# An mLSTM and two feed-forward layers on one core: state products of two batches in one group, a planner's constants, and the weights' conversion on VectorE and ScalarE alone

## The chip, the core and the metric

The kernel runs on one core of a Trainium2 chip. The core has TensorE for matrix products (PE in the profile, with its weight loads as PEld), VectorE (DVE), ScalarE (ACT), GpSimd (POOL) and SyncE (SP), which here issues every DMA. The metric is the device time of one execution in microseconds; less is better.

## The reference

A recurrence over 768 steps for 4 batches and 8 heads of size 40 gives `y`; two feed-forward layers of width 320 and inner width 2048 follow, all in float32.

```python
for t in range(S):                                  # S = 768, per batch and head
    m_new = maximum(f[t] + m, i[t])
    fs, is_ = exp(f[t] + m - m_new), exp(i[t] - m_new); m = m_new
    C = fs * C + is_ * outer(v[t], k[t])            # 40 x 40 state
    n = fs * n + is_ * k[t]
    y[t] = sigmoid(o_gate[t]) * (C @ q[t]) / maximum(abs(n @ q[t]), 1)
x = y.reshape(3072, 320)
h = x @ w_in1;  x = maximum(0.01 * h, h) @ w_out1   # layer 0
h = maximum(x @ w_in2, 0);  out = (h * h) @ w_out2  # layer 1
```

## The kernel before

**Work.** Time is cut into 6 chunks of 128 steps, and a chunk of all 4 batches is a block of 512 tokens. `attention(c)` computes a chunk in parallel form: for each of 8 groups `g` (a batch, four heads) decay factors (`ex_`, L626, then a triangular `affine_select` on GpSimd, L629), the products of keys and queries (`mS`, L635), their product with the factors on VectorE (L638), the product with the values (`mPV`, L651, or `mPV3` in three bf16 parts, L657 to L660), and from chunk 1 on the part from the state (`mI`, L645). For each batch the state is renewed: GpSimd weights the values (`wv`, L696), `mU` (L705) multiplies them with the keys for 8 heads into the PSUM tile `attm`, and VectorE adds (L719). Then come the gates (L732 to L739), a transposition (`mT`, L746) and the split of the block into a rounded and a low part, `xH` and `xL` (L752). Keys and values of a batch lie in a tile `nat` with two slots, `wv` has two slots too, and `attm` is one bank that `mU` and `mT` share.

**Feed-forward layers.** For each block and each of 16 slices `j` of the inner width, `moe_h` makes 8 products into `hp` (L435), ScalarE and VectorE make of it `gH` and its low part `gL` (L441 to L443, in layer 1 L446 to L449), and `out1` (L466 to L472) or `out2` (L514 to L516) adds its 8 or 12 products to accumulators. Chunk 0 of layer 0 is done in two halves of 256 tokens, the second seven slices behind the first, since its 16 weight slices arrive and are converted in the meantime.

**Conversion.** `weight(layer, j)` gets a slice as raw 64-bit words (704 KB) and makes a rounded and a low part: a shift and a merge on VectorE (L394, L396), a conversion of the low words on ScalarE (L398), an addition (L399), the rounding on ScalarE (L402), and subtractions for the low parts (`stack`, 64 x 128, L411; `sub`, L406, for layer 0 of 512 and of 64 columns). Addition and subtractions can go to VectorE or GpSimd: the planner decides by which is free first.

**Order.** Each operation is handed to `Sched` with an engine, an assumed duration and a key, the time in hundredths of a block at which it should come. `Sched.order` plays these operations through on a model of the engines, turns the plan into latest times, does so six times and keeps the best plan. Each engine then runs its instructions in that order. The keys are built from the numbers of `ORDER`: for instance `w0` and `ws` set those of the weights of layer 0, `c0` and `cs` those of the attention of the next chunk, `a04`, `a1` and others those of the first two chunks. While the planner finds nothing for TensorE early in the program, it places products of zeros (L322, L462, L479).

Of the kernel before, what the change touches and what calls it, by code (L numbers as in the profile page):

```python
# [19 lines left out]
E = 42  # L20
# [30 lines left out]
class Sched:  # L51
# [211 lines left out]
def mlstm_moe_kernel(  # L263
# [111 lines left out]
    def weight(layer, j, key):  # L375
        if layer == 0:
            raw = sb(f"x2_{(4, 5, 0, 1)[j % 4]}", [128, WR, 2], I32)
            if j < 2:
                fs[j] = sb(f"x2_{2 + j}", [128, 2, WR], I32)
            fb, fr = fs[j % 2], j // 2 % 2  # L380
        else:
            raw = sb(("T", "X")[j % 2], [128, WR, 2], I32)
            fb, fr = sb("qkr", [128, 1, WR], I32), 0
        ft = lambda: fb.t[:, fr]
        w = sb(f"w{j}", [128, WT], F32R)
        wt[layer, j] = w
# [4 lines left out]
        op("DVE", dve(WR, True), key, lambda: V.tensor_scalar(out=ft(), in0=hi(), scalar1=3, scalar2=0x3FFFFFFF, op0=ALU.logical_shift_left, op1=ALU.bitwise_and),  # L394
           r=[(raw, 0)], w=[(fb, fr)])
        op("DVE", dve(WR), key, lambda: V.scalar_tensor_tensor(out=ft(), in0=hi(), scalar=-0x40000000, in1=ft(), op0=ALU.bitwise_and, op1=ALU.bitwise_or),  # L396
           r=[(raw, 0), (fb, fr)], w=[(fb, fr)])
        op("ACT", act(WR), key - 0.1, lambda: A.activation(l.t, raw.t.bitcast(U32)[:, :, 0], AF.Copy, scale=2.0 ** -29), r=[(raw, 0)], w=[(l, 0)])  # L398
        add = lambda eng: eng.tensor_tensor(out=ft(), in0=ft(), in1=l.t, op=ALU.add)  # L399
        op("DVE", dve(WR), key, lambda: add(V), r=[(fb, fr), (l, 0)], w=[(fb, fr)], alt=("POOL", pool(WR), lambda: add(G)))  # L400
        f32 = lambda: ft().bitcast(F32)
        op("ACT", act(WR), key, lambda: A.copy(w.t[:, 0:WR], f32()), r=[(fb, fr)], w=[(w, "H"), (w, "C")])  # L402
        c0 = 512 if layer == 0 else 576

        def low(eng, o, n, s):
            eng.tensor_tensor(out=w.t[:, o:o + n], in0=f32()[:, s:s + n], in1=w.t[:, s:s + n].bitcast(F32), op=ALU.subtract)  # L406


        def stack(eng):
            c = w.t[64:128, c0:c0 + 128]  # L410
            eng.tensor_tensor(out=c, in0=f32()[64:128, c0:c0 + 128], in1=c.bitcast(F32), op=ALU.subtract)  # L411

        op("DVE", dve(128), key, lambda: stack(V), r=[(fb, fr), (w, "C")], w=[(w, "C")], alt=("POOL", pool(128), lambda: stack(G)))
        def sub(o, n, s0, w_):
            op("DVE", dve(n), key, lambda: low(V, o, n, s0), r=[(fb, fr), (w, "H")], w=w_, alt=("POOL", pool(n), lambda: low(G, o, n, s0)))

        if layer == 0:
            sub(768, 512, 0, [(w, "L")])
            sub(704, 64, 640, [(w, "Lc")])
        else:  # L420
            sub(704, 576, 0, [(w, "L"), (w, "Lc")])
# [108 lines left out]
    def attention(c, keys, ld):  # L530
# [31 lines left out]
        if c == 0:  # L562
            op("ACT", 100, -499, lambda: A.activation(act0.t, act0.t, AF.Exp), r=[(act0, 0)] + [(ogt, b) for b in range(B)], w=[(act0, 0)], table="exp")

        for b in range(B):
            kb = keys[2 * b] + (10 if c == 0 else 0)
            nt = sb("nat", [128, H * D + H * E], slots=2)
# [125 lines left out]
            if c < NCH - 1:  # L693
                kU = ko + (0.8 if c else 8 if b > 1 else 185)
                wv = sb("wv", [128, H, E], slots=2)
                mwv = lambda eng, wv=wv, v=v, b=b: eng.tensor_tensor(  # L696
                    out=wv.t, in0=v(), in1=ex.t[:, 1, 8 * b:8 * b + 8].unsqueeze(2).to_broadcast([128, H, E]), op=ALU.mult)
                op("POOL", 708, kU - 0.2, lambda mwv=mwv: mwv(G), r=[(nt, 0), (ex, 0)], w=[(wv, 0)])
                ks = kU + ORDER["ks"] if c == 0 else ko + 2
                up = ps("attm")  # L700

                def mU(up=up, wv=wv, nt=nt):
                    for h in range(H):
                        r, o = h % 2 * 64, h // 2 * E
# [3 lines left out]
                st = lambda b=b: C32.t[:, 8 * b:8 * b + 8]
                stk = lambda k, b=b: C32.t[:, 8 * b + k:8 * b + 8:2]
                u = lambda k, up=up: up.t[64 * k:64 * k + D, 0:H // 2 * E].rearrange("p (h e) -> p h e", e=E)  # L710
                if c == 0:
                    for k in range(2):
                        op("ACT", act(H // 2 * E, True), kU, lambda stk=stk, u=u, k=k: A.copy(stk(k), u(k)), r=[(up, 0)], w=[(C32, (b, k))])
                else:
                    op("POOL", 708, ko + 0.7, lambda st=st, b=b: G.tensor_tensor(
                        out=st(), in0=st(), in1=ex.t[0:D, 2, 8 * b:8 * b + 8].unsqueeze(2).to_broadcast([D, H, E]), op=ALU.mult),
                        r=[(ex, 0), (C32, (b, 0)), (C32, (b, 1))], w=[(C32, (b, 0)), (C32, (b, 1))])
                    for k in range(2):
                        op("DVE", dve(H // 2 * E), kU, lambda stk=stk, u=u, k=k: V.tensor_tensor(out=stk(k), in0=stk(k), in1=u(k), op=ALU.add),  # L719
                           r=[(up, 0), (C32, (b, k))], w=[(C32, (b, k))])  # L720
                if c + 1 >= NATIVE:
                    rb = slice(8 * b, 8 * b + 8)
                    CL = sb("CL", [D, H, E], F32R, 2)
                    op("ACT", act(H * E), ks, lambda st=st, rb=rb: A.copy(Cst.t[0:D, rb], st()), r=[(C32, (b, 0)), (C32, (b, 1))], w=[(Cst, (b, 0))])
                    op("DVE", dve(H * E), ks, lambda st=st, rb=rb, CL=CL: V.tensor_tensor(
                        out=CL.t, in0=st(), in1=Cst.t[0:D, rb].bitcast(F32), op=ALU.subtract), r=[(C32, (b, 0)), (C32, (b, 1)), (Cst, (b, 0))], w=[(CL, 0)])
                    op("SP", 800, ks, lambda rb=rb: SP.dma_start(out=Cst.t[2 * D:3 * D, rb].bitcast(F32), in_=Cst.t[0:D, rb].bitcast(F32)), r=[(Cst, (b, 0))], w=[(Cst, (b, 2))], lat=300)
                    op("SP", 800, ks, lambda rb=rb, CL=CL: SP.dma_start(out=Cst.t[D:2 * D, rb].bitcast(F32), in_=CL.t.bitcast(F32)), r=[(CL, 0)], w=[(Cst, (b, 1))], lat=300)
# [126 lines left out]
```

## Time and profile before

| | |
|---|---|
| median of 3 runs | 869.04 us (864.34 to 873.08) |
| profiled execution | 863.92 us, of which the span is 862.2 us |
| granted clock of TensorE, mean | 0.994 |
| TensorE busy | 843.5 us (98%) |
| VectorE, ScalarE, GpSimd busy | 540.1, 465.7, 115.1 us |

A row of the profile groups equal instructions: line, engine, operation, result and operands, count, then busy time and the mean of one in ns, then the idle time of the engine just before them and what ended it. The start of a matrix product is exact, its end is modelled; the time of a group of products is read from one group's start to the next.

### The profile page before, as it was taken

To read this page: it belongs to the slowest core of one execution; us is meant where nothing else is said; L and a number is where in the kernel's file an instruction comes from. 1 tells how busy PE (TensorE), PEld (TensorE's weight loads), DVE (VectorE), ACT (ScalarE), POOL (GpSimd) and SP (SyncE) were. 2 spreads that over 40 slices of the span, in tenths; PEclk is the share of its full clock that TensorE was granted. 3 is DMA by queue.
4 is the path that set the end of the run, shared out by engine and by line. 5 is a ranking of instruction groups with operands and counts; after the bars stand their busy time and mean duration, and the time that the engine had idled before them with its cause. 6 is when DMAs were issued, how large, how long until landed. Compare 5 with 4: busy or idle time off the path is not lost.

```text
span 862.2 us, 14025 instructions
## 1 busy us (share of the span) xinstructions
PE 843.5 (98%) x5307; PEld 723.9 (84%) x5311; DVE 540.1 (63%) x967; ACT 465.7 (54%) x946; POOL 115.1 (13%) x142
## 2 busy tenths in 40 slices
PE   9989999999999999999999999999999999999998
PEld 7788899777777778778777889999999999999997
DVE  5999946766866777667666899453443443533433
ACT  7577537755865685587546665443333433433332
POOL 2566614100310310011100000000000000000000
PEclk9899999999999999999999999999999999999999
DMA  8686224444444444452232442000000000000000
GB/s 226 215 264 196 70 62 153 137 128 126 142 132 131 140 130 133 129 163 94 93 115 100 136 160 76 1 31 1 1 31 1 0 32 1 31 1 1 32 1 31
DMA packets 52212, 78.61 MB, mean 91 GB/s; under 512 B 4336, under 2 KB 40784, under 8 KB 52144
## 3 DMA queue, kind: packets, MB, share of 16 engines
q1 hardware_dynamic: 52144, 77.71, 28.2%
q8 instruction: 42, 0.69, 0.3%
q14 instruction: 26, 0.21, 0.1%
HBM read 54.26 MB, written 4.01 MB: 68 GB/s over the span
## 4 chain that ended last, share of the span: by engine, by line
PE 76%; DVE 10%; ACT 5%; issue 3%; DMA 2%; SPq 2%; POOL 1%; ACTq 0%; POOLq 0%; DVEq 0%
PE hp L435 35%; PE acc L466 4%; PE acc L468 3%; PE acc L516 3%; PE acc L467 3%; PE acc L515 3%; PE acc L514 3%; SPq L581 2%; PE acc L471 2%; PE acc L472 2%; PE atty L645 2%; PE attS L635 2%; DVE aw L638 1%; PE atty L516 1%; PE atty L514 1%
## 5 line engine op out<-in xcount | busy, mean ns | idle before, releaser
L435 PE MATMUL hp<-xH,w 128*128 128x512 f32 (+1 forms) x1040 | 295.6, 381 | 6.9 <-DVE gL L443 3.6
L435 PEld LDWEIGHTS hp<-xH,w 128*128 128x128 f32 x1040 | 183.4, 189 | 38.3 <-DVE gL L443 5.5
L435 PE MATMUL hp<-xL,w 128*128 128x512 f32 (+1 forms) x624 | 198.6, 375 | 0.0
L447 DVE TENSOR_TENSOR g<-g 128x512 f32<-128x512 f32 x96 | 67.5, 704 | 117.9 <-ACT g L446 117.9
L435 PEld LDWEIGHTS hp<-xL,w 128*128 128x128 f32 x624 | 115.6, 189 | 22.4
L446 ACT ACTIVATE g<-hp 128x512 f32<-128x512 f32 x96 | 57.3, 597 | 128.9 <-PE hp L435 128.9
L449 DVE TENSOR_TENSOR gL<-g,gH 128x512 fp32r<-128x512 f32 x96 | 66.4, 692 | 57.1 <-ACT gH L448 57.1
L448 ACT CAST gH<-g 128x512 fp32r<-128x512 f32 x96 | 59.5, 620 | 71.7 <-DVE g L447 71.7
L466 PE MATMUL acc<-gH,w 128*128 128x512 f32 (+1 forms) x224 | 86.7, 387 | 0.0
L441 ACT ACTIVATE gH<-hp 128x512 fp32r<-128x512 f32 (+1 forms) x112 | 59.4, 532 | 49.7 <-PE hp L435 39.4
L443 DVE TENSOR_TENSOR gL<-hp,gH 128x512 fp32r<-128x512 f32 (+1 forms) x112 | 68.1, 609 | 28.3 <-ACT hp L442 27.4
L468 PE MATMUL acc<-gL,w 128*128 128x512 f32 (+1 forms) x224 | 81.2, 363 | 0.8 <-DVE gL L443 0.8
L467 PE MATMUL acc<-gH,w 128*128 128x512 f32 (+1 forms) x224 | 80.8, 361 | 0.0
L516 PE MATMUL acc<-w,gL 128*128 128x320 f32 x192 | 59.3, 309 | 0.0
L515 PE MATMUL acc<-w,gH 128*128 128x320 f32 x192 | 59.3, 309 | 0.0
L514 PE MATMUL acc<-w,gH 128*128 128x320 f32 x192 | 59.2, 308 | 0.0
L442 ACT ACTIVATE hp<-hp 128x512 f32<-128x512 f32 (+1 forms) x112 | 58.9, 528 | 0.0
L629 POOL TENSOR_SCALAR_AFFINE_SELECT aw<-aw 128x512 f32<-128x512 f32 x48 | 34.5, 719 | 170.5 <-ACT aw L626 168.3
L626 ACT ACTIVATE aw<-aw,cs 128x128 f32<-128x128 f32 x160 | 50.7, 392 | 11.6 <-DMA aw<-Adram 11.4
L468 PEld LDWEIGHTS acc<-gL,w 128*128 128x128 f32 x224 | 42.4, 189 | 7.8 <-DVE gL L443 1.0
L466 PEld LDWEIGHTS acc<-gH,w 128*128 128x128 f32 x224 | 42.5, 190 | 5.4 <-DVE x L485 0.4
L467 PEld LDWEIGHTS acc<-gH,w 128*128 128x128 f32 x224 | 42.5, 190 | 4.3
(167 smaller groups left out, 1540.8 us busy)
## 6 DMA issues: line engine op xcount, KB each, us to landing
T<-X SPq DMA_DIRECT2D x144, 120.0 KB
x<-in_wts_dram SPq DMA_DIRECT2D x16, 704.0 KB
aw<-Adram SPq DMA_DIRECT2D x40, 256.0 KB
nat<-in_nat_dram SPq DMA_DIRECT2D x24, 328.0 KB
qkr<-in_qk_dram SPq DMA_DIRECT2D x16, 360.0 KB
X<-in_wts_dram SPq DMA_DIRECT2D x8, 704.0 KB
T<-in_wts_dram SPq DMA_DIRECT2D x8, 704.0 KB
og<-in_og_dram SPq DMA_DIRECT2D x12, 320.0 KB
```

The lines of the kernel that those rows point to most:

```text
L435: T.matmul(hp.t[:, 0:n], w.t[:, col:col + 128], x.t[:, kt, o], start=(s == 0), stop=(s == 7))
L441: op("ACT", act(n, True), key, lambda: A.activation(gH.t[:, 0:n], h(), AF.Prelu, alpha=0.01), r=[(hp, 0)], w=[(gH, 0)])
L443: op("DVE", dve(n), key, lambda: V.tensor_tensor(out=gL.t[:, 0:n], in0=h(), in1=gH.t[:, 0:n].bitcast(F32), op=ALU.subtract), r=[(hp, 0), ( ...
L447: op("DVE", dve(n), key, lambda: V.tensor_tensor(out=g.t, in0=g.t, in1=g.t, op=ALU.mult), r=[(g, 0)], w=[(g, 0)])
L448: op("ACT", act(n), key, lambda: A.copy(gH.t, g.t), r=[(g, 0)], w=[(gH, 0)])
L449: op("DVE", dve(n), key, lambda: V.tensor_tensor(out=gL.t, in0=g.t, in1=gH.t.bitcast(F32), op=ALU.subtract), r=[(g, 0), (gH, 0)], w=[(gL, 0)])
L466: T.matmul(a[t].t[:, o], w.t[:, hc:hc + 128], gH.t[:, 0:n], start=first, stop=False)
L467: T.matmul(a[t].t[:, o], w.t[:, lc:lc + 128], gH.t[:, 0:n], start=False, stop=False)
L468: T.matmul(a[t].t[:, o], w.t[:, hc:hc + 128], gL.t[:, 0:n], start=False, stop=last)
L514: T.matmul(a.t[:, 0:DM], gH.t[:, s], wH, start=first, stop=False)
L515: T.matmul(a.t[:, 0:DM], gH.t[:, s], wL, start=False, stop=False)
L516: T.matmul(a.t[:, 0:DM], gL.t[:, s], wH, start=False, stop=last)
```

## The change

Three things change. First, `mU` takes two batches at a time: it is issued after the second of a pair, has 16 products into two halves of one `attm` bank, and reads both `nat` and both `wv` tiles. What follows it (copies or additions, split, DMAs) stays as it was for each batch. Second, the alternatives on GpSimd for the addition and the subtractions of the weights' conversion are taken out. Third, twelve of the numbers of `ORDER` are other ones. Lines behind the deleted one are one lower (L406 is L405, L435 is L434), those behind the pair's code four higher (L746 is L750); `mU` is at L708.

```diff
-ORDER = dict(... kv=-5.41, ... z=-8.14, ... o0=1.33, a04=-6.78, a0s=5.39, a1=30.61, a1s=6.5, ... w0=-23.81, ws=2.43, bias=0.88, c0=-7.4, cs=11.88, cld=28.29, ...)
+ORDER = dict(... kv=-2.33, ... z=-15.1, ... o0=1.85, a04=-6.78, a0s=4.65, a1=29.4, a1s=5.72, ... w0=-33.49, ws=2.64, bias=1.13, c0=-19.03, cs=13.0, cld=31.54, ...)
...
-        add = lambda eng: eng.tensor_tensor(out=ft(), in0=ft(), in1=l.t, op=ALU.add)
-        op("DVE", dve(WR), key, lambda: add(V), ..., alt=("POOL", pool(WR), lambda: add(G)))
+        op("DVE", dve(WR), key, lambda: V.tensor_tensor(out=ft(), in0=ft(), in1=l.t, op=ALU.add), ...)
...
-        op("DVE", dve(128), key, lambda: stack(V), ..., alt=("POOL", pool(128), lambda: stack(G)))
+        op("DVE", dve(128), key, lambda: stack(V), ...)
...
-            op("DVE", dve(n), key, lambda: low(V, o, n, s0), ..., alt=("POOL", pool(n), lambda: low(G, o, n, s0)))
+            op("DVE", dve(n), key, lambda: low(V, o, n, s0), ...)
...
+                pair = pair[-1:] + [(b, wv, nt)] if b % 2 else [(b, wv, nt)]
+            if c < NCH - 1 and b % 2:
                 up = ps("attm")
-                def mU(up=up, wv=wv, nt=nt):
-                    for h in range(H):
-                        r, o = h % 2 * 64, h // 2 * E
-                        T.matmul(up.t[r:r + D, o:o + E], nt.t[:, h * D:(h + 1) * D], wv.t[:, h], start=True, stop=True)
-                op("PE", 730, kU, mU, r=[(nt, 0), (wv, 0)], w=[(up, 0)])
+                def mU(up=up, pair=pair):
+                    for i, (_, wv, nt) in enumerate(pair):
+                        for h in range(H):
+                            r, o = h % 2 * 64, (4 * i + h // 2) * E
+                            T.matmul(up.t[r:r + D, o:o + E], nt.t[:, h * D:(h + 1) * D], wv.t[:, h], start=True, stop=True)
+                op("PE", 1170, kU, mU, r=[(x, 0) for _, wv, nt in pair for x in (wv, nt)], w=[(up, 0)])
```

The planner's output changes on every engine. The program has 20 groups `mU` before and 10 after; 142 instructions on GpSimd before and 41 fewer after, which stand on VectorE; 37 and 36 products of zeros.

SyncE, the first transfers of the program (`x_0_74` holds the gates, `w_..` with `in_qk_dram` queries and keys of chunk 0, `nat` keys and values, `og` the output gates, `x_4_122` and `x_5_126` raw weights), before and after:

```order
L311 DMA x_0_74<-in_gates_dram 32x2x128
L604 DMA w_88<-in_qk_dram 40x1024
L604 DMA w_91<-in_qk_dram 40x1024
L568 DMA nat<-in_nat_dram 128x656
L604 DMA w_100<-in_qk_dram 40x1024
L604 DMA w_103<-in_qk_dram 40x1024
L559 DMA og<-in_og_dram 128x640 x2
L568 DMA nat<-in_nat_dram 128x656
L311 DMA x_0_74<-in_gates_dram 32x2x640
L387 DMA x_4_122<-in_wts_dram 128x1408
```

```order
L311 DMA x_0_74<-in_gates_dram 32x2x128
L604 DMA w_88<-in_qk_dram 40x1024
L604 DMA w_91<-in_qk_dram 40x1024
L568 DMA nat<-in_nat_dram 128x656
L311 DMA x_0_74<-in_gates_dram 32x2x640
L604 DMA w_102<-in_qk_dram 40x1024
L604 DMA w_105<-in_qk_dram 40x1024
L558 DMA og<-in_og_dram 128x640 x2
L568 DMA nat<-in_nat_dram 128x656
L387 DMA x_4_122<-in_wts_dram 128x1408
```

The second part of the gates goes ahead of two transfers of queries and keys, the output gates and a `nat`.

VectorE, around the low parts of the last weight slice of layer 0 (`w_1283` before, `w_1392` after; `w_1267` and `w_1329` are the two slices before it), before and after:

```order
L739 TENSOR_TENSOR y<-hs,og 128x320
L638 TENSOR_TENSOR aw<-aw,attS 128x512
L406 TENSOR_TENSOR w_1283<-x_3_417,w_1283 128x512
L406 TENSOR_TENSOR w_1283<-x_3_417,w_1283 128x64
L725 TENSOR_TENSOR CL<-C_69,Cst 40x336
L752 TENSOR_TENSOR xL<-attm,xH 128x3x128
```

```order
L743 TENSOR_TENSOR y<-hs,og 128x320
L638 TENSOR_TENSOR aw<-aw,attS 128x512
L405 TENSOR_TENSOR w_1267<-x_3_338,w_1267 128x64
L405 TENSOR_TENSOR w_1392<-x_3_338,w_1392 128x512
L410 TENSOR_TENSOR w_1392<-x_3_338,w_1392 64x128
L405 TENSOR_TENSOR w_1329<-x_2_289,w_1329 128x64
L405 TENSOR_TENSOR w_1392<-x_3_338,w_1392 128x64
L729 TENSOR_TENSOR CL<-C_69,Cst 40x336
```

All low parts now stand in VectorE's row, those of 64 columns a slice or two behind the others. Up to and with the last low part of 512 columns VectorE's row holds, before and after: 8 and 16 additions (L399), 3 and 15 of `stack`, 14 and 16 low parts of 512 columns, 1 and 14 of 64, 18 and 20 of `gL` (L443, after L442), 13 and 15 of L638.

TensorE, a state product in layer 0 (`w_..` is a weight slice, `acc_..` an accumulator), before and after:

```order
L468 MATMUL acc_1968<-gL,w_546 128x512
L471 MATMUL acc_1979<-gH,w_546 128x512
L472 MATMUL acc_1979<-gL,w_546 128x512
L705 MATMUL attm<-wv,nat 40x42 x8
L435 MATMUL hp<-xH,w_686 128x512 x4
L435 MATMUL hp<-xL,w_686 128x512 x2
```

```order
L470 MATMUL acc_2007<-gH,w_386 128x512
L471 MATMUL acc_2007<-gL,w_386 128x512
L635 MATMUL attS<-T 128x128 x4
L708 MATMUL attm<-wv,nat 40x42 x16
L645 MATMUL atty<-Cst,T 128x42 x4
L434 MATMUL hp<-xH,w_583 128x512 x4
```

One group of 16 stands where two of 8 stood, and in this place inside the attention's row instead of between two groups of the feed-forward layer. In TensorE's row the 19th of the 32 half-block groups `moe_h` of chunk 0 comes before the change behind 18 x 8 products L435, 120 products of `out1`, 48 of `mS`, 16 of `mI`, 48 of `mPV` and 15 transpositions; the 24th comes after the change behind 23 x 8, 155, 60, 28, 60 and 21.

## Rows read from the trace of the kernel before

**Rows 1.** The page, busy time, share of the span and instructions of each engine.

```profile
PE 843.5 (98%) x5307; PEld 723.9 (84%) x5311; DVE 540.1 (63%) x967; ACT 465.7 (54%) x946; POOL 115.1 (13%) x142
```

**Rows 2.** Busy time by stretch; the last columns are granted clock, DMA share, GB/s.

```profile
14.40:103.50 89.10, 81.67 (x657) 72.07 (x659) 87.39 (x150) 63.80 (x154) 56.12 (x59) 0.94 0.60 191
103.50:155.00 51.50, 51.24 (x451) 48.29 (x450) 29.05 (x67) 29.29 (x74) 11.70 (x17) 1.00 0.35 107
```

**Rows 3.** Groups of VectorE between 14.4 and 103.5 us.

```profile
L406 DVE TENSOR_TENSOR w<-x,w 128x512 fp32r<-128x512 f32 x14 | 13.3, 956 | 0.0
L394 DVE TENSOR_SCALAR x<-x 128x704 int32<-128x704 int32 x16 | 11.1, 712 | 0.0
...
L733 DVE TENSOR_SCALAR d<-d 128x8 f32<-128x8 f32 x6 | 2.8, 467 | 0.0
```

**Rows 4.** Groups of VectorE from 103.5 us to the end.

```profile
L399 DVE CUSTOM_DVE_ANT_0 qkr<-qkr,wl 128x1408 uint16<-128x1408 uint16 x15 | 13.3, 888 | 0.3
L406 DVE TENSOR_TENSOR w<-qkr,w 128x576 fp32r<-128x576 f32 x16 | 12.4, 775 | 0.2
...
L411 DVE TENSOR_TENSOR w<-qkr,w 64x128 fp32r<-64x128 f32 x15 | 4.3, 290 | 7.3 <-ACT w L402 7.2
L394 DVE TENSOR_SCALAR qkr<-X 128x704 int32<-128x704 int32 x8 | 4.2, 525 | 0.2
...
L733 DVE TENSOR_SCALAR d<-d 128x8 f32<-128x8 f32 x18 | 4.0, 224 | 0.5
```

**Rows 5.** Groups of GpSimd between 14.4 and 103.5 us.

```profile
L399 POOL TENSOR_TENSOR x<-x,wl 128x704 int32<-128x704 int32 x8 | 15.6, 1950 | 4.6 <-DVE x L396 3.6 <-ACT wl L398 0.8
L411 POOL TENSOR_TENSOR w<-x,w 64x128 fp32r<-64x128 f32 x13 | 10.4, 803 | 8.5 <-ACT w L402 7.7 <-POOL wv L696 0.3
...
L406 POOL TENSOR_TENSOR w<-x,w 128x64 fp32r<-128x64 f32 x15 | 9.6, 645 | 2.0 <-ACT w L402 1.4
...
L406 POOL TENSOR_TENSOR w<-x,w 128x512 fp32r<-128x512 f32 x2 | 2.6, 1284 | 0.7 <-ACT w L402 0.6
```

**Rows 6.** Timeline of GpSimd and of VectorE at 40 us: start, duration, instruction.

```profile
40.01 1.76 POOL L399 TENSOR_TENSOR x<-x,wl 128x704 int32<-128x704 int32 x1 [0.83 <-ACT wl L398]
...
40.17 1.64 DVE L733 TENSOR_SCALAR d<-d 128x8 f32<-128x8 f32 x1
```

**Rows 7.** Timeline of VectorE, 10 to 14.5 us; in brackets the idle time before.

```profile
10.56 0.69 DVE L638 TENSOR_TENSOR aw<-aw,attS 128x512 f32<-128x512 f32 x1 [5.25 <-PE attS L635]
11.16 0.68 DVE L638 TENSOR_TENSOR aw<-aw,acc 128x512 f32<-128x512 f32 x1
12.54 0.47 DVE L348 TENSOR_TENSOR_SCAN T<-x,T 32x128 f32<-32x128 f32 x1 [0.70 <-DMA x<-in_gates_dram]
14.44 0.69 DVE L638 TENSOR_TENSOR aw<-aw,attS 128x512 f32<-128x512 f32 x1 [1.42 <-PE attS L635]
```

**Rows 8.** Timeline of TensorE, 104 to 115 us.

```profile
104.22 0.64 PE L435 MATMUL hp<-xH,w 128*128 128x256 f32 x4
...
106.14 0.64 PE L435 MATMUL hp<-xH,w 128*128 128x256 f32 x4
...
111.03 1.16 PE L635 MATMUL attS<-X 40*128 40x128 f32 x8
112.03 0.98 PE L645 MATMUL atty<-C,X 40*128 40x42 f32 x8
112.94 0.51 PE L705 MATMUL attm<-wv,nat 128*40 128x42 f32 x16
113.38 1.09 PE L651 MATMUL atty<-nat,aw 128*128 128x42 f32 x8
```

**Rows 9.** Timeline of TensorE at a state product in layer 0.

```profile
161.96 0.39 PE L471 MATMUL acc<-gH,w 128*128 128x512 f32 x1
162.19 0.39 PE L472 MATMUL acc<-gL,w 128*128 128x512 f32 x1
162.50 0.51 PE L705 MATMUL attm<-wv,nat 128*40 128x42 f32 x16
```

More of the change, by code (lines that the diff above doesn't have):

```diff
@@ L29 @@
 AMIN = -110.0
-ORDER = dict(pe0=7000, ld2=80, kv=-5.41, ks=6.4, g2=32.54, z=-8.14, lag=7, m0=0.71, o0=1.33, a04=-6.78, a0s=5.39, a1=30.61, a1s=6.5, a1ld=23.83, w0=-23.81, ws=2.43, bias=0.88, c0=-7.4, cs=11.88, cld=28.29, wl=1.51, outk=2.04)
+ORDER = dict(pe0=7000, ld2=80, kv=-2.33, ks=6.4, g2=32.54, z=-15.1, lag=7, m0=0.71, o0=1.85, a04=-6.78, a0s=4.65, a1=29.4, a1s=5.72, a1ld=23.83, w0=-33.49, ws=2.64, bias=1.13, c0=-19.03, cs=13.0, cld=31.54, wl=1.51, outk=2.04)
 SHARE = 0.6
@@ L398, in weight @@
         op("ACT", act(WR), key - 0.1, lambda: A.activation(l.t, raw.t.bitcast(U32)[:, :, 0], AF.Copy, scale=2.0 ** -29), r=[(raw, 0)], w=[(l, 0)])
-        add = lambda eng: eng.tensor_tensor(out=ft(), in0=ft(), in1=l.t, op=ALU.add)
-        op("DVE", dve(WR), key, lambda: add(V), r=[(fb, fr), (l, 0)], w=[(fb, fr)], alt=("POOL", pool(WR), lambda: add(G)))
+        op("DVE", dve(WR), key, lambda: V.tensor_tensor(out=ft(), in0=ft(), in1=l.t, op=ALU.add), r=[(fb, fr), (l, 0)], w=[(fb, fr)])
         f32 = lambda: ft().bitcast(F32)
@@ L411, in stack @@
             eng.tensor_tensor(out=c, in0=f32()[64:128, c0:c0 + 128], in1=c.bitcast(F32), op=ALU.subtract)
-        op("DVE", dve(128), key, lambda: stack(V), r=[(fb, fr), (w, "C")], w=[(w, "C")], alt=("POOL", pool(128), lambda: stack(G)))
+        op("DVE", dve(128), key, lambda: stack(V), r=[(fb, fr), (w, "C")], w=[(w, "C")])
         def sub(o, n, s0, w_):
-            op("DVE", dve(n), key, lambda: low(V, o, n, s0), r=[(fb, fr), (w, "H")], w=w_, alt=("POOL", pool(n), lambda: low(G, o, n, s0)))
+            op("DVE", dve(n), key, lambda: low(V, o, n, s0), r=[(fb, fr), (w, "H")], w=w_)
         if layer == 0:
@@ L563, in attention @@
             op("ACT", 100, -499, lambda: A.activation(act0.t, act0.t, AF.Exp), r=[(act0, 0)] + [(ogt, b) for b in range(B)], w=[(act0, 0)], table="exp")
+        pair = []
         for b in range(B):
@@ L707, in attention @@
-                op("PE", 730, kU, mU, r=[(nt, 0), (wv, 0)], w=[(up, 0)])
[L708 to L728, printed above, removed]
+                def mU(up=up, pair=pair):
[3 more added lines that the diff above has]
+                            T.matmul(up.t[r:r + D, o:o + E], nt.t[:, h * D:(h + 1) * D], wv.t[:, h], start=True, stop=True)
@@ new lines, in attention @@
+                op("PE", 1170, kU, mU, r=[(x, 0) for _, wv, nt in pair for x in (wv, nt)], w=[(up, 0)])
+                for i, (b2, _, _) in enumerate(pair):
+                    st = lambda b=b2: C32.t[:, 8 * b:8 * b + 8]
+                    stk = lambda k, b=b2: C32.t[:, 8 * b + k:8 * b + 8:2]
+                    u = lambda k, up=up, i=i: up.t[64 * k:64 * k + D, 4 * i * E:(4 * i + 4) * E].rearrange("p (h e) -> p h e", e=E)
+                    if c == 0:
+                        for k in range(2):
+                            op("ACT", act(H // 2 * E, True), kU, lambda stk=stk, u=u, k=k: A.copy(stk(k), u(k)), r=[(up, 0)], w=[(C32, (b2, k))])
+                    else:
+                        op("POOL", 708, ko + 0.7, lambda st=st, b=b2: G.tensor_tensor(
+                            out=st(), in0=st(), in1=ex.t[0:D, 2, 8 * b:8 * b + 8].unsqueeze(2).to_broadcast([D, H, E]), op=ALU.mult),
+                            r=[(ex, 0), (C32, (b2, 0)), (C32, (b2, 1))], w=[(C32, (b2, 0)), (C32, (b2, 1))])
+                        for k in range(2):
+                            op("DVE", dve(H // 2 * E), kU, lambda stk=stk, u=u, k=k: V.tensor_tensor(out=stk(k), in0=stk(k), in1=u(k), op=ALU.add),
+                               r=[(up, 0), (C32, (b2, k))], w=[(C32, (b2, k))])
+                    if c + 1 >= NATIVE:
+                        rb = slice(8 * b2, 8 * b2 + 8)
+                        CL = sb("CL", [D, H, E], F32R, 2)
+                        op("ACT", act(H * E), ks, lambda st=st, rb=rb: A.copy(Cst.t[0:D, rb], st()), r=[(C32, (b2, 0)), (C32, (b2, 1))], w=[(Cst, (b2, 0))])
+                        op("DVE", dve(H * E), ks, lambda st=st, rb=rb, CL=CL: V.tensor_tensor(
+                            out=CL.t, in0=st(), in1=Cst.t[0:D, rb].bitcast(F32), op=ALU.subtract), r=[(C32, (b2, 0)), (C32, (b2, 1)), (Cst, (b2, 0))], w=[(CL, 0)])
+                        op("SP", 800, ks, lambda rb=rb: SP.dma_start(out=Cst.t[2 * D:3 * D, rb].bitcast(F32), in_=Cst.t[0:D, rb].bitcast(F32)), r=[(Cst, (b2, 0))], w=[(Cst, (b2, 2))], lat=300)
+                        op("SP", 800, ks, lambda rb=rb, CL=CL: SP.dma_start(out=Cst.t[D:2 * D, rb].bitcast(F32), in_=CL.t.bitcast(F32)), r=[(CL, 0)], w=[(Cst, (b2, 1))], lat=300)
```

## The prediction, made before the changed kernel ran

> **What bounds the kernel now.** The page comes first: TensorE is busy for 843.5 of 862.2 us and no other engine passes 63% [rows 1], so only time in which TensorE waits, goes slow or multiplies zeros can be won. The table by stretch says where that is. From 14.4 to 103.5 us, while the first layer's weights arrive and are converted, TensorE is busy for 81.67 of 89.1 us, with a granted clock of 0.94, and VectorE for 87.39 us of 89.1, which is full; from 103.5 us on VectorE has room (29.05 of 51.5 us) and TensorE has none (51.24) [rows 2]. So until 103.5 us, when the last weight slice is converted, VectorE sets the pace, and afterwards TensorE does. What counts is therefore when VectorE is through with the weights, and how much of TensorE's fixed work has been done by then.
>
> Within that stretch VectorE is slower than it is elsewhere. L394 takes 712 ns there and 525 later; L733, on 8 columns, 467 and 224; L406 takes 956 ns for 512 columns and later 775 for 576 [rows 3, 4]. The reason stands in one pair of rows: an addition on GpSimd runs from 40.01 for 1.76 us, and L733 on VectorE, started at 40.17, ends with it at 41.8 [rows 6]. GpSimd was busy for 56.12 us of the stretch [rows 2].
>
> **The weights' conversion without GpSimd: what VectorE gets.** Up to the last low part of 512 columns its row holds 8 more additions at 0.89 us (7.1), 12 more of `stack` at 0.29 (3.5) and 2 more low parts of 512 columns [rows 4]; 775 ns for 576 columns is about 0.71 for 512 (1.4). The undisturbed price of the 13 low parts of 64 columns is in no row; it lies under the 0.29 us of 128 columns and above zero, and since 64 columns cost 0.07 us in the step from 512 to 576, I take 0.22 (2.9; ends 0 and 3.8). Attention has also moved ahead of that point: 2 products L638 at 0.69 [rows 7], 2 of `gL`, and ten shorter ones, 4.5 us together by estimate. That is 19.4 us; successive starts lie closer than the durations (0.60 us apart for 0.69 [rows 7]), which for 40 instructions takes off 3.4: **16.0 us more**.
>
> **What VectorE is spared.** L406 loses 14 x (0.956 - 0.71) = 3.4 us to the collisions, L394 16 x (0.712 - 0.525) = 3.0 and L733 6 x (0.467 - 0.224) = 1.5 [rows 3, 4], together 7.9 us in 36 of the 150 instructions. The later rows hold collisions too, and the other groups lose as well, so that is a lower end; the upper is the 56.1 us of GpSimd itself. The 36 hold 27.2 of VectorE's 87.39 us and lose 29% of it; many of the others read PSUM, as L638 with its 0.69 us [rows 7], and I give the other 60 us a tenth, which makes 14 us in all, nearer to the lower end. The conversion is 15.6 + 10.4 + 9.6 + 2.6 = 38.2 us of GpSimd's time [rows 5], or 68% of it, so **9.5 us are freed** (at least 5.4; nothing at all is a rival below).
>
> The Trainium skill (SBUF — State Buffer, on who shares a port with whom) says that VectorE and GpSimd hold a common pair of ports as an exclusive lock, and that of VectorE's instructions only those with two SBUF inputs or in a two-port mode meet it. Rows 6 agree with a full block. The rule speaks against the change in one point: the rows that move to VectorE have two SBUF inputs, so what stays on GpSimd, the triangular selects and `wv`, would meet VectorE more often, and by that the time would be that of rival (b) below.
>
> **What starts earlier.** VectorE is idle for 5.25 + 0.70 + 1.42 = 7.4 us before 14.4 us, among them for the gates' second part, which is used at 12.54 us [rows 7]. In the new row of SyncE that transfer goes out fifth instead of ninth or tenth, ahead of two of queries and keys, the output gates and a `nat`, and VectorE does the gates' scans before its first L638 instead of behind it. At least one wait, for TensorE's first scores, stays. Of 7.4 us I take **5.0** as used (ends 0 and 7.4). What is put behind the gates pays little: the first weight slice is the next in SyncE's row as it was.
>
> So VectorE would finish the last slice at 103.5 + 16.0 - 9.5 - 5.0 = 105.0 us, 1.5 us later than before.
>
> **What TensorE gets done beside it.** That is the planner's part, and the larger one. Before, TensorE began its 19th half-block group at 104.2 us [rows 8], just as the last slice was ready; after, the 24th, which is the first to need that slice, is the place that matters. By the counts of the two rows it has then done 40 more products L435 and 35 more of `out1`, which take 0.12 us each (16 from 104.22 to 106.14), 12 heads of `mS` at 0.25 (1.00 us for four), 12 of `mI` and 12 of `mPV` at 0.23 (0.91 for four) [rows 8], and 2 transpositions of 0.3: 9.0 + 3.0 + 2.7 + 2.7 + 0.6 = **18.0 us** of work that used to come after 103.5. The work as a whole is the same, so the end comes 18.0 - 1.5 = 16.5 us earlier if TensorE is there in time. It won't be fully: the more evenly the two engines are matched, the more each waits in its fixed order for the other. Before, TensorE idled 7.4 us in the stretch while VectorE waited 1.7 us [rows 2]; I set 5.0 us (ends 0 and 12) for new waits, on VectorE for rounding on ScalarE above all. **11.5 us** remain.
>
> **The state products.** Alone a group lasts 0.44 us (112.94 to 113.38 [rows 8]), and behind a product of the feed-forward layer it begins 0.31 us after that instead of 0.23 [rows 9]. Its 16 products last 0.51 us with their pipeline's end of some 0.21 us, so the starts span 0.30 and about 0.12 us is drained at the end. Entry and end together are 0.20 us, and one of two is saved ten times: **2.0 us** (ends 0, and 4.4 if a second group came free). The 16 products of a pair stay on TensorE's path, since that engine is full. The wait that is added is for the second batch's `wv`, on GpSimd, and behind `mU` in TensorE's row stand the state's part `mI` and the next feed-forward group; the stage around it has GpSimd idle for most of the time [rows 1], so I cost it at nothing. Both `nat` slots are held until the pair is done, so the next two loads go together and later; twenty microseconds of feed-forward groups stand in the row before their first use, and if that cover were gone each of the ten pairs would add what its load takes.
>
> **The sum.** 11.5 + 2.0 = 13.5 us. The profiled execution took 863.92 us with a span of 862.2, and would become 850.4. The three runs have their median 5.1 us higher, at 869.04, which gives **855.5 us**. About 1%, or 8.7 us, is what a measurement of this kernel can tell from no change.
>
> **Rivals.** (a) *TensorE is in time*: no new waits and all of the idle 7.4 us used. Then 18.0 + 0.9 + 2.0 = 20.9 us are won, 848 us. For it speaks that the new order puts each slice's low parts a steady distance ahead of their use; against it, that six different engines and queues would have to keep a plan's times. (b) *The collisions stay*: what GpSimd keeps meets the longer row of VectorE as often as the conversion did, and nothing of the 9.5 us is freed. The last slice is ready at 114.5 us, and 18.0 - 11.0 - 5.0 + 2.0 = 4.0 us remain: 865 us. For it speaks that the moved instructions are themselves of the kind that is blocked. (c) *VectorE as a worse bound, slower than before*: the collisions stay, and in its fixed row VectorE also waits for ScalarE twice in each of 16 slices, as it does in the second layer's conversion for L402, 7.2 us in 15 slices or 0.48 us each [rows 4]. That is 15.4 us in place of my 5.0; the slice is ready at 129.9 us, 26.4 later than before, and 26.4 - 18.0 - 2.0 = 6.4 us are lost: 875 us. It decides from the point where VectorE finishes later than 123.5 us. (d) *The planned order does not come about*: TensorE stands at the 24th group no earlier than before (its work beside VectorE is held up by something the rows don't show, a late weight transfer for instance), and only the state products remain: 867 us.
>
> **How the numbers follow.** The forecast, with all that lies between 850 and 860 us, gets 0.53; (a), 0.15; (b) and (d), 0.24 together; (c) 0.08, of which half lies above 877.7. The range should leave out no more than 2 in 10: 847 to 868 us takes in most of (a), (b) and (d). Faster by over 1% means below 860.3: the forecast, (a), and none of the others, 0.68; within 1%, 0.26; slower by over 1%, 0.06.
>
> **What would show it.** In the new profile VectorE's last low part of 512 columns near 105 us and GpSimd busy for about 18 us between 14 and 105; L394 near 0.55 us and L733 near 0.25 in that stretch; VectorE's first long wait ended before 8 us; the 24th half-block group of TensorE begun between 104 and 110 us, against a 19th at 104.2 before; ten state groups of about 0.78 us. From the end of chunk 0 on the two traces should run alike. The prediction is wrong if VectorE shows waits for ScalarE of more than 10 us before its last slice, if L394 stays at 0.7 us, if TensorE stands idle at `nat` or at the pairs, or if the clock is held low for longer than before.

## The result and the profile after

The changed kernel took 856.33 us, the median of 4 runs (854.75 to 859.1), against 870.12 us for the kernel before (4 runs, 864.34 to 873.08). The ratio is 0.9864, 95% interval 0.9815 to 0.9913. The forecast was 855.5 us. The profiled execution took 857.15 us with a span of 855.1, only 7.1 us less than the 862.2 of the profiled execution of before; the medians lie 13.8 us apart. That gap is the first thing to explain. One run, of the kernel with pairs and conversion but the old numbers, took 1041.99 us at a mean clock of 0.736 and is left out of that kernel's median and ratio below.

Engines of the page after, which answers to [rows 1]:

```profile
PE 842.0 (98%) x5310; PEld 729.9 (85%) x5310; DVE 541.4 (63%) x1008; ACT 464.9 (54%) x946; POOL 77.8 (9%) x101
```

The table by stretch after, as in [rows 2], and the groups of VectorE from 14.4 to 103.5 us, as in [rows 3]:

```profile
14.40:103.50 89.10, 86.25 (x670) 77.24 (x670) 81.64 (x170) 62.49 (x153) 21.10 (x23) 0.89 0.62 195
103.50:155.00 51.50, 51.18 (x438) 48.06 (x437) 36.12 (x84) 33.44 (x85) 12.07 (x15) 1.00 0.42 123
```

```profile
L405 DVE TENSOR_TENSOR w<-x,w 128x512 fp32r<-128x512 f32 x14 | 10.7, 761 | 0.4 <-ACT w L401 0.2
L394 DVE TENSOR_SCALAR x<-x 128x704 int32<-128x704 int32 x15 | 8.2, 554 | 0.0
```

The collisions went: L394 takes 554 ns instead of 712, GpSimd is busy for 21 us instead of 56, and VectorE, with 20 instructions more, is no longer full. (In the second execution of before, shown below, VectorE is busy for 81.71 us of the stretch as well, so it is not full in every execution of before.) But TensorE's granted clock is 0.89 in the stretch instead of 0.94. The timeline of VectorE after at the start (with [rows 7]) and at the last weight slice:

```profile
7.83 0.47 DVE L348 TENSOR_TENSOR_SCAN T<-x,T 32x128 f32<-32x128 f32 x1 [2.54 <-DMA x<-in_gates_dram]
...
12.50 0.67 DVE L638 TENSOR_TENSOR aw<-aw,attS 128x512 f32<-128x512 f32 x1
...
112.36 0.68 DVE L405 TENSOR_TENSOR w<-x,w 128x512 fp32r<-128x512 f32 x1
```

The gates' second part is used at 7.83 us instead of 12.54, after a wait of 2.54 us; before, the wait that VectorE began at the same point lasted 5.25 us and was for TensorE's scores. The last low part of 512 columns begins at 112.36 us and is done at 113.0, not near 105. In the timeline of TensorE after, the 24th half-block group, a state pair in chunk 0, one behind which TensorE waits, the first product of the first full block and layer 1's first `out2`:

```profile
88.77 0.81 PE L708 MATMUL attm<-wv,nat 128*40 128x42 f32 x32
89.51 0.38 PE L465 MATMUL acc<-gH,w 128*128 128x256 f32 x1
...
117.79 0.64 PE L434 MATMUL hp<-xH,w 128*128 128x256 f32 x4
...
144.80 0.74 PE L434 MATMUL hp<-xH,w 128*128 128x512 f32 x2
...
199.49 0.81 PE L708 MATMUL attm<-wv,nat 128*40 128x42 f32 x32
201.06 0.59 PE L645 MATMUL atty<-Cst,T 120*128 120x42 f32 x4 [0.75 <-DVE hs L686]
...
511.73 0.30 PE L513 MATMUL attS<-w,gH 128*128 128x320 f32 x1
```

The same two marks stand at 143.30 and 518.80 us in the profiled execution of before:

```profile
143.30 0.93 PE L435 MATMUL hp<-xH,w 128*128 128x512 f32 x3
...
518.80 0.30 PE L514 MATMUL attS<-w,gH 128*128 128x320 f32 x1
```

So against that execution chunk 0 won nothing (144.80 against 143.30), and the stage from the first full block to layer 1, where I had expected both traces to run alike, went from 375.5 to 366.9 us. From layer 1's first `out2` to the end both take 343.4 us.

### The profile page after: what moved, and what is told of

It is laid out like the page before. It is cut to its first block, busy times and chain, and to the rows that moved or that the text cites. A ratio compares the mean times of both kernels' runs of the same rounds, so it can differ in the third digit from the quotient of the medians.

```text
span 855.1 us, 14028 instructions
## 1 busy us (share of the span) xinstructions
PE 842.0 (98%) x5310; PEld 729.9 (85%) x5310; DVE 541.4 (63%) x1008; ACT 464.9 (54%) x946; POOL 77.8 (9%) x101
## 4 chain that ended last, share of the span: by engine, by line
PE 82%; DVE 6%; ACT 4%; SPq 3%; DMA 3%; issue 1%; ACTq 0%; DVEq 0%
PE hp L434 36%; PE acc L465 4%; PE acc L467 4%; PE acc L466 4%; SPq L581 3%; PE acc L515 3%; PE acc L514 3%; PE acc L513 3%; PE attS L635 3%; PE acc L470 2%; PE atty L645 2%; PE acc L471 2%; PE atty L651 2%; DMA T<-X 2%; PE atty L515 1%
## 5 line engine op out<-in xcount | busy, mean ns | idle before, releaser
L434 PE MATMUL hp<-xH,w 128*128 128x512 f32 (+1 forms) x1040 | 294.8, 381 | 0.3 <-DVE gL L442 0.3
L434 PEld LDWEIGHTS hp<-xH,w 128*128 128x128 f32 x1040 | 183.5, 189 | 29.2 <-DVE gL L442 0.9
L434 PE MATMUL hp<-xL,w 128*128 128x512 f32 (+1 forms) x624 | 199.1, 375 | 0.0
L434 PEld LDWEIGHTS hp<-xL,w 128*128 128x128 f32 x624 | 115.9, 189 | 22.4
L442 DVE TENSOR_TENSOR gL<-hp,gH 128x512 fp32r<-128x512 f32 (+1 forms) x112 | 68.3, 610 | 34.7 <-ACT hp L441 34.2
L626 ACT ACTIVATE aw<-aw,cs 128x128 f32<-128x128 f32 x160 | 50.8, 391 | 12.2 <-DMA aw<-Adram 12.1
```

The source lines that it names most:

```text
L434: T.matmul(hp.t[:, 0:n], w.t[:, col:col + 128], x.t[:, kt, o], start=(s == 0), stop=(s == 7))
L442: op("DVE", dve(n), key, lambda: V.tensor_tensor(out=gL.t[:, 0:n], in0=h(), in1=gH.t[:, 0:n].bitcast(F32), op=ALU.subtract), r=[(hp, 0), ( ...
```

## The experiments

Three theories were set against each other: V, my own (VectorE's relief beside the weights); O (the new order after chunk 0); and K (part of the difference is TensorE's clock, which differs from execution to execution).

### The kernel before, once more

No edit. 

> The kernel before, once more, as a control. Theory V (VectorE's relief beside the weights explains the gain) and theory O (the gain is the new order of attention among the feed-forward groups after 150 us) both expect 864 to 873 us, ratio 1 within 0.006. Theory K (the spread of the kernel before, 864 to 873 us, is time at half clock, and so part of the 13.8 us between the medians is the clock and not the change) expects the runs' granted clocks to differ: a clock lower by 0.004 is 6.9 us more at half speed and should cost at most 3.4 us; a run at 873 us should show 0.984 or less. If all runs show 0.990 to 0.994 and still spread over 8 us, K falls.

Measured: 871.51 us, median of 10 runs (864.21 to 874.55), ratio 1.0011 (0.9975 to 1.0047). Its profiled execution has a span of 870.9 us. Here is the table by stretch, 16 to 30 us, of three executions: the first profile of before, this one, and after (the clock is the third number from the end):

```profile
16.00:30.00 14.00, 13.17 (x84) 9.39 (x85) 13.06 (x27) 8.39 (x25) 7.66 (x7) 0.76 0.59 164
```

```profile
16.00:30.00 14.00, 13.78 (x70) 11.35 (x70) 8.95 (x18) 7.74 (x21) 5.14 (x5) 0.51 0.54 152
```

```profile
16.00:30.00 14.00, 14.00 (x66) 10.76 (x66) 9.84 (x23) 7.79 (x20) 1.53 (x2) 0.51 0.79 229
```

One program, two clocks: 0.76 and 0.51 in the same 14 us. The reader can see the cost in VectorE's column: 13.06 us of work where the clock was higher, 8.95 where TensorE ran at 1.2 GHz. The first full block begins at 151.92 us here, not 143.30, while the stage behind it takes 375.6 us in this one (151.92 to 527.49) and 375.5 in the first:

```profile
151.92 0.93 PE L435 MATMUL hp<-xH,w 128*128 128x512 f32 x3
...
527.49 0.30 PE L514 MATMUL attS<-w,gH 128*128 128x320 f32 x1
```

Over 59 runs of this program (the ten here and those taken beside every experiment), the 16 with a mean clock of 0.986 average 873.3 us and the 22 with 0.992 average 867.8: 5.4 us for 0.006, or 2 x 0.006 x 868 = 10.4 us more at half clock. A line through all runs gives 0.56 us per us at half clock, a little over K's bound of one half. At 0.992 alone they still spread from 863.8 to 871.6, so the amount of half clock is not all of it. K stands for much of the spread and for the small difference between the two profiles that I compared first: the profile that the prediction was made from was one of the fastest executions.

### Only the engine of the conversion, at a fixed order

Before's order, with the conversion that it puts on GpSimd issued on VectorE in the same place:

```diff
-... alt=("POOL", pool(WR), lambda: add(G)))
+... alt=("POOL", pool(WR), lambda: add(V)))
-... alt=("POOL", pool(128), lambda: stack(G)))
+... alt=("POOL", pool(128), lambda: stack(V)))
-... alt=("POOL", pool(n), lambda: low(G, o, n, s0)))
+... alt=("POOL", pool(n), lambda: low(V, o, n, s0)))
```

> The order of before, every row as planned there, but the additions and subtractions that the plan gives to GpSimd are issued on VectorE in the same place. Theory V: VectorE is the bound up to 103.5 us; it gets 8 additions at 0.89, 13 stack at 0.29, 2 low parts at 0.71 and 15 of 64 columns at about 0.2, some 15 us, and is spared 9.5 us of collisions, so its last slice comes some 5 us later and, TensorE's order being the old one, the whole takes 872 to 878 us. If the collisions were worth no more than VectorE's own price differences in rows (7.9 us), 875 to 880. Theory O: nothing in chunk 0 decides the time, 866 to 872 us, same as before within 0.5%. Both: L394 about 0.53 and L733 about 0.2 us between 14 and 103 us.

Measured: 871.29 us, ratio 1.0036 (1.0005 to 1.0067). The stretch from 14.4 to 103.5 us and VectorE's groups in it, in the control and here:

```profile
14.40:103.50 89.10, 80.60 (x632) 71.26 (x636) 81.71 (x144) 63.20 (x152) 50.70 (x58) 0.92 0.61 191
...
L406 DVE TENSOR_TENSOR w<-x,w 128x512 fp32r<-128x512 f32 x13 | 12.9, 1000 | 0.0
L394 DVE TENSOR_SCALAR x<-x 128x704 int32<-128x704 int32 x16 | 12.0, 772 | 0.0
L399 DVE CUSTOM_DVE_ANT_0 x<-x,wl 128x1408 uint16<-128x1408 uint16 x7 | 7.1, 1016 | 0.0
L411 DVE TENSOR_TENSOR w<-x,w 64x128 fp32r<-64x128 f32 x3 | 1.4, 457 | 0.1
```

```profile
14.40:103.50 89.10, 81.16 (x613) 72.09 (x617) 82.83 (x172) 60.80 (x144) 16.55 (x20) 0.88 0.58 185
...
L399 DVE CUSTOM_DVE_ANT_0 x<-x,wl 128x1408 uint16<-128x1408 uint16 x15 | 13.2, 882 | 2.2 <-ACT wl L398 2.2
L406 DVE TENSOR_TENSOR w<-x,w 128x512 fp32r<-128x512 f32 x15 | 10.7, 710 | 0.1
L394 DVE TENSOR_SCALAR x<-x 128x704 int32<-128x704 int32 x15 | 7.5, 524 | 0.1
L406 DVE TENSOR_TENSOR w<-x,w 128x64 fp32r<-128x64 f32 x13 | 4.2, 319 | 0.0
L411 DVE TENSOR_TENSOR w<-x,w 64x128 fp32r<-64x128 f32 x14 | 4.1, 290 | 0.9 <-ACT w L402 0.5
```

By the second fence's prices VectorE got 8 x 0.88 + 11 x 0.29 + 13 x 0.32 + 2 x 0.71 = 15.8 us more, and its busy time in the stretch went from 81.71 to 82.83 us. Part of that small rise is work that slid out of the stretch. Instruction by instruction, the 144 that the control's VectorE has in the stretch took 11.4 us less here, so some 11 us of collisions went with GpSimd's work, most of what VectorE spent on the work itself; the last of the 144 begins at 105.39 us instead of 102.88. By the ratio the time rose by 3 us (0.4 to 5.8); the median lies in O's range and just below V's.

The other way round, after's order with 36 instructions back on GpSimd in the same place:

```diff
-... lambda: V.tensor_tensor(out=ft(), in0=ft(), in1=l.t, op=ALU.add), ...
+... lambda: (G if layer == 0 and j % 2 == 0 else V).tensor_tensor(out=ft(), in0=ft(), in1=l.t, op=ALU.add), ...
-... lambda: stack(V), ...
+... lambda: stack(G if layer == 0 and j < 13 else V), ...
-... lambda: low(V, o, n, s0), ...
+... lambda: low(G if layer == 0 and j < 15 and n == 64 else V, o, n, s0), ...
```

> The order of the kernel after, every row as planned there, but 8 additions, 13 stack and 15 low parts of 64 columns of layer 0 are issued on GpSimd again in the same place. Theory V (collisions cost more than the moved rows' price on VectorE): the last low part of 512 columns comes later than after's and the time is 862 to 868 us. Theory O (the two nearly cancel, as in the order of before, where moving them to VectorE cost 0.4%): 853 to 859 us, VectorE's long rows back at 0.65 to 0.7 for L394.

Measured: 857.2 us (4 runs), ratio 0.9844 (0.9789 to 0.9899): not to be told from after. VectorE is busy for 73.53 us of the stretch instead of 81.64 and L394 is back at 723 ns. At a fixed order the engine of the conversion is worth at most a few us in either direction, and V, in the size that I gave it, falls.

### Parts of the numbers, and the two edits without them

All twelve numbers on the kernel before: the line `ORDER` of the diff, nothing else. 

> The kernel before with the new numbers of ORDER alone; state products single, conversion still shared with GpSimd. Theory V: the collisions stay, VectorE stays full, 865 to 870 us. Theory O: nearly the whole gain, less 2 us for the single state products: 857 to 861 us, and between 150 us and the end of layer 0 the trace shortens by 5 us or more against before.

Measured: 859.17 us (4 runs), ratio 0.9884 (0.9841 to 0.9927), inside O's range. The stage from the first full block to layer 1 takes 368.5 us (145.64 to 514.10).

Pairs and conversion without the numbers: the diff without its `ORDER` line. 

> Pairs and conversion without GpSimd, with the old numbers of ORDER. Theory V: VectorE is relieved as after, though the order around it is another: 856 to 864 us. Theory O: only the pairs' 2 us and no better order: 865 to 872 us.

Measured: 866.53 us (nine runs, 862.52 to 874.51), ratio 0.9953 (0.9920 to 0.9985). O's range holds it. By the medians, the numbers alone give 1.2%, the two edits alone 0.5%, all together 1.4 to 1.6%, close to a sum. But the clock was low longest of all profiles here, 0.973, and over the nine runs 29 us on average were at half clock, against 17.9 in before's 59. At like clocks the two edits are worth more: the two runs at 0.986 took 863.68 and 865.05 us, where before's 16 average 873.3, so the parts together exceed the whole. The stage from the first full block to layer 1 is shorter too, 372.1 us (157.27 to 529.38), without any of the numbers.

Three of the numbers, then the other nine:

```diff
-ORDER = dict(... c0=-7.4, cs=11.88, cld=28.29, ...)
+ORDER = dict(... c0=-19.03, cs=13.0, cld=31.54, ...)
```

> The kernel before with three new numbers alone: c0, cs and cld, which set when the attention of the next chunk comes among the feed-forward groups and when its loads go out. All twelve together gave 859.2 us. Theory O (the gain is made after chunk 0): these three carry it, 860 to 864 us, and from the first full block of 512 tokens to layer 1's first out2 the trace takes 367 to 370 us instead of the 375.5 of before. Theory V (the gain is made beside the weights): 867 to 871 us.

> The kernel before with the other nine new numbers (kv, z, o0, a0s, a1, a1s, w0, ws, bias), which set chunk 0's attention, weights and half-block groups. Theory O: little, 866 to 871 us. Theory V: 860 to 864 us, with the end of chunk 0 some 8 us earlier than the control's 159.1 us for the last half-block product, less what the clock differs.

Measured: the three 880.92 us, ratio 1.0109 (1.0047 to 1.0170), slower than before; the nine 863.82 us, ratio 0.9941 (0.9913 to 0.9969). Both theories missed with the three; with the nine V's range holds the time and O's does not. Most of what the three lose is likely the clock: their four runs show 0.978 to 0.986, and the one at 0.986 took 873.62 us, as before's do at that clock. Their stage takes 378.3 us (157.99 to 536.25), 2.7 more than the control's, and the waits of TensorE in it (who, for whom: us, times, longest) show the attention of the next chunk coming before VectorE is ready for it:

```profile
PE atty L645 <- DVE hs L686: 3.7, 7, 0.9
PE attS L635 <- DVE aw L638: 2.3, 3, 1.1
PE attm L746 <- DVE y L739: 1.7, 3, 0.8
```

With the nine alone the stage takes 372.4 us (146.45 to 518.84), with all twelve 368.5; the rest of what the nine gain lies in chunk 0. The numbers work as a set: which of them carries the stage can't be read from parts, since any edit gives the planner another order everywhere.

### Each edit undone, and after once more

State products single again, all else as after (the old `mU` and its operation). 

> The kernel after with the state products of each batch alone again, as in before. By the rows a pair group costs 0.744 us from its start to the next and a single one 0.437, so ten pairs save 1.3 us, and ten entries of 0.08 us, 2.1 us in all: 857.5 to 860 us. Rival (the planner's whole order, which shifts with any edit, decides more than the edit): the time lies over 3 us away from that on either side, and the difference lies in a stage in which the products' own time has not changed.

GpSimd's alternatives back, all else as after. 

> The kernel after with the alternatives on GpSimd back in the conversion, which the planner then uses. Theory V: 860 to 866 us, since VectorE is full again up to 103 us. Theory O (the conversion's engine is worth nothing, as with a_conv_pool at after's order): 854 to 860 us.

After itself, no edit. 

> The kernel after once more, as a control and for a closer ratio. Theory K (half clock costs about 0.5 us for each us of it, in whichever execution): its runs spread over 854 to 860 us with their clocks between 0.982 and 0.996, median 855.5 to 858 us, ratio to before 0.983 to 0.989. If the clock explained the difference between the medians, runs of before and of after at one granted clock (0.992) would lie within 4 us of each other; theory O expects 11 to 13 us there.

Measured side by side, median of 6 runs each, before at 871.98 us:

| kernel | us | ratio (95%) | mean clock, profiled | first full block | to layer 1 |
|---|---|---|---|---|---|
| after | 856.43 | 0.9844 (0.9795 to 0.9893) | 0.992 | 144.10 | 366.8 |
| single state products | 857.41 | 0.9871 (0.9825 to 0.9918) | 0.996 | 142.07 | 368.5 |
| GpSimd's alternatives back | 859.71 | 0.9892 (0.9847 to 0.9937) | 0.992 | 146.71 | 366.2 |

The intervals of the ratios overlap, but the runs themselves say more. All six with GpSimd back (858.11 to 862.41) lie above all six of after (853.96 to 857.83), so that edit's 3.3 us are clear of the spread. Without the pairs the medians differ by 1.0 us, but four of its six runs have a clock of 0.994 to 0.996, which none of after's reach; its two at 0.986 and 0.988 took 861.08 and 861.74 us, where after's two at 0.988 took 857.15 and 857.83. The pairs are likely worth 3 to 4 us at like clocks, on few runs. The stage agrees for after with the first profile (366.9). Without the pairs it is 1.7 us longer; by a count of the products inside it, its order holds about 1 us more of TensorE's work from outside, so that is no sure gain of the pairs. With GpSimd back the stage is as short as after's, and the loss lies in chunk 0 (146.71 against 144.10, at the same mean clock): the edit is worth something there through the order that the planner then builds, not at a fixed one. After's ten runs average 856.3 us and before's 59 runs 869.6, with 16.6 and 17.9 us at half clock, and at a clock of 0.992 before averages 867.8 (22 runs) and after 855.6 (2 runs). So the clock does not explain the difference of the medians; O's 11 to 13 us at one clock hold.

### Holding the clock up

After's order, with products of zeros behind TensorE's groups that are planned between 8 and 18 us: behind each (twelve in the end, not eleven), or behind every second one (six).

```diff
             n.fn()
+            if n.eng == "PE" and n.seq >= 0 and 8000 <= n.start < 18000:
+                product()
```

> The order of the kernel after with eleven more products of zeros (128x512, bf16), one behind each group of TensorE planned between 8 and 18 us. Theory K (the half clock from 16.1 to 29.7 us costs TensorE up to 3.4 us, in which VectorE waits for it): the granted clock stays at 1.00 for longer after 16 us, the first half-block group begins at 32 to 34 us instead of 35.4, and the time is 852 to 856 us. Rival: TensorE has no room between 8 and 16 us; the eleven cost 0.22 us each, 2.4 us, and the clock falls all the same: 857 to 861 us.

> The order of after with half of the added products of zeros of clock_fill, six between 8 and 18 us. Theory K: the clock stays at 2.4 GHz past 16 us with six as well, mean granted clock 0.994 or more, and TensorE has 1.3 us less to do than in clock_fill: 853.5 to 855 us, faster than both. Rival: six are too few, the clock falls at about 16 us for 13 us as in after: 855.5 to 858 us.

Measured: twelve, 854.93 us (4 runs), ratio 0.9832 (0.9786 to 0.9878), profiled clock 0.998. Six, 853.55 us (6 runs, 851.65 to 862.31), ratio 0.9829 (0.9777 to 0.9882), profiled clock 1.000. The table by stretch of the second, and its TensorE at the first half-block group and at layer 1:

```profile
16.00:30.00 14.00, 11.89 (x108) 8.61 (x106) 13.34 (x29) 10.15 (x27) 3.47 (x4) 1.00 0.86 244
```

```profile
31.67 0.72 PE L434 MATMUL hp<-xH,w 128*128 128x256 f32 x4
...
506.42 0.30 PE L513 MATMUL attS<-w,gH 128*128 128x320 f32 x1
```

The clock stays at 2.4 GHz, VectorE gets 13.34 us of work done in those 14 instead of 9.84, and the first half-block group begins at 31.67 us instead of 35.39. The best profiled span is 849.8 us. In one of the six runs the clock fell all the same (0.985, 862.3 us), and the interval overlaps after's, so the 2.9 us of the medians are likely rather than shown. That the products hold the clock up is clearer: nine of these ten runs show 0.994 or more, none of after's ten more than 0.992. With six it is the fastest kernel of the study.

## Why the number was right, and its place wrong

**The number.** 855.5 us forecast, 856.3 and 856.4 measured: within the range, and faster by over 1%. It came out right by luck, through terms that erred in opposite directions.

**"From the end of chunk 0 on the two traces should run alike."** This step failed, and it is the larger part of the gain. The stage shrank from 375.5 and 375.6 us in two executions of before to 366.9 and 366.8 in two of after, some 8.7 us at full clock in all four; by a count of the products, about 1 us of it is attention that after has done before the mark. The twelve numbers alone bring 7.1. The two edits without the numbers shorten the stage as well (372.1), so it is not the numbers' alone. What shrinks is shown in part. Read from start to start, first profile of before against after, 6.5 us of it go by behind the 1320 products of the feed-forward layer, which are the same in both (318.3 and 311.8 us), and 2.9 us behind the 48 transpositions (7.0 and 4.1); the other products of attention come out 0.9 us longer. TensorE's waits in the stage, first in the control and then after:

```profile
PE attS L635 <- DVE aw L638: 1.8, 5, 0.5
PE hp L435 <- ACT xH L751: 1.8, 2, 0.9
PE atty L645 <- DVE hs L686: 1.2, 3, 0.5
PE attm L746 <- DVE y L739: 0.8, 2, 0.5
```

```profile
PE atty L645 <- DVE hs L686: 2.7, 4, 0.8
PE atty L659 <- DVE x L665: 1.6, 2, 1.3
PE attS L635 <- DVE aw L638: 1.1, 2, 0.8
PE attm L750 <- DVE y L743: 0.2, 1, 0.2
```

The two waits at the end of an attention, for the split `xH`, are gone, and with the rows left out here the listed waits fall from 6.8 us in 15 to 5.6 in 9. The rest I can only argue: TensorE turns from feed-forward groups to attention 102 times in the stage before and 88 times after, and an entry costs 0.08 us [rows 9], 1.1 us in all, besides what drains. Why the other entries got shorter stays open. I had read the numbers of `ORDER` for chunk 0 alone, though three of those that changed (`c0`, `cs`, `cld`) are about the later chunks, and had looked at the orders there only for the state products.

**"TensorE gets 18.0 us more done."** The step rests on a miscount. The group at 104.22 us [rows 8] is the 20th, not the 19th, which began here:

```profile
98.89 0.75 PE L435 MATMUL hp<-xH,w 128*128 128x256 f32 x4 [1.48 <-DVE gL L443]
```

The difference between the 20th and the 24th is 8 products L435 less, 8 of `out1`, 4 each of `mS`, `mI` and `mPV` and one transposition of three products, 5.1 us by my own prices; 12.9 would have been left, and the sum would have said 861 us. Its place was not right either: the mark that should have come at 104 to 110 us came at 117.79.

**"VectorE would finish the last slice at 105.0."** It finished at 113.0. Up to there VectorE was busy for 9.98 us before 14.4 us and 90.90 behind, against 5.20 and 87.39 up to 103.5 before: 8.3 us more work, where I had 6.5. The other 6 us are idle time: 12.2 us in all against 10.9, where I had taken off 5.0.

**"VectorE gets 16.0, is spared 9.5."** The conversion's part of the first was 14.9 us before I took off the overlap, and 15.8 at a fixed order. The second was somewhat small (some 11 us there), so the conversion cost VectorE some 3 to 4 us. Rival (b), that what stays on GpSimd would meet the longer row as often, is refuted: L394 fell to 554 ns, and to 524 with before's order. The Trainium skill (SBUF — State Buffer, Who interferes with whom) gave this rival its ground; the port pair that it names agrees with the rows, the consequence that I drew from it does not.

**"5.0 used of the start."** The gates came early as said (7.83 us, with the first L638 behind them), and up to 14.4 us VectorE was busy for 4.8 us more than before. But from 16 us on TensorE ran at 1.2 GHz until 30 us and became the engine that VectorE waits for: 9.84 us of VectorE's work in 14. The clock was on my list of what would prove the sum wrong, and it had no term in it. At equal clocks chunk 0 did gain, by an estimated 1 to 5 us: after ends it at 144.10 with a mean clock of 0.992 and at 144.80 with 0.988, and a line through before's two executions (143.30 at 0.994, 151.92 at 0.986) gives 145.5 and 149.8 there.

**"The state products, 2.0."** A pair takes 0.74 us to the next group's start, a single one 0.44 [rows 8], so ten pairs save 1.3 us and ten entries 0.8, as said. But "I cost the added wait at nothing" failed: behind three of the ten pairs TensorE waits for VectorE, as at 199.49 us, where 1.57 us go by instead of 0.74; the other two take 1.14 and 1.61. That is 2.1 us; behind the single products of the run without pairs no wait stands in that stage. What the pairs bring all the same, 1.0 us by the medians and perhaps 3 to 4 at like clocks, comes with another order and can't be told from it.

## What to carry to other kernels

Before a sum is made against one profiled execution, find out how its time stands to others of the same program, and look at the granted clock by stretch: a profile of a lucky execution hides a term. A scheduler's constants act everywhere, so compare the two orders at each stage of the program and not only where the edits are. To price an edit under a planner, make it at a fixed order: there the conversion on VectorE cost 0.4% or nothing, while with the planner's order around it the same edit gained 0.4%. And set times beside each other at like clocks: the two edits alone seemed worth 0.5%, and about 1% where the clocks agreed.

## What the runs showed of the hardware

TensorE's clock fell although TensorE did not pause: in after's profile it was busy for 14.95 of the first 16 us, without a gap from 1.05 us on, yet from 16 to 30 us the granted clock is 0.51, which is the lower level of 1.2 GHz for nearly all of it.

```profile
0.00:16.00 16.00, 14.95 (x90) 10.83 (x91) 11.58 (x27) 8.70 (x19) 4.64 (x11) 1.00 0.83 242
```

What preceded the fall, from 7 us on, were products of at most 128 columns; with six products of 512 columns added, three of them before 16 us (10.71, 13.11 and 15.04), it stayed at 2.4 GHz in the profiled execution. The Trainium skill (TensorE: Matmul & The Clock Gate, Part 1) says that activity releases the throttle and idleness brings it back; here an engine that shows as busy was throttled. Nor is it the same from one execution to the next: 0.76 and 0.51 in one stretch of one program.

The price of the collision of VectorE and GpSimd, at before's order: GpSimd's work in the stretch fell from 50.70 to 16.55 us, and the 144 instructions of VectorE that are the same in both took 11.4 us less, a third of that. Some 7 us of it are those of L394 and L406; the rest is spread over many rows.
